# Attention with a top-32 mask, then experts: score tiles as pairs of 64-row products, token rows copied by ScalarE and multiplied by GpSimd

## The chip, the cores and the metric

The kernel runs on one core of a Trainium2 chip. The metric is the time of one execution in device microseconds (us). Five engines work side by side, each through its own instructions in order: PE (TensorE, matrix products), DVE (VectorE), ACT (ScalarE), POOL (GpSimd) and SP (SyncE, which here only issues DMAs). They meet through semaphores. PE reads SBUF and writes PSUM; DVE and ACT read both; POOL works on SBUF alone.

## The reference, cut to what matters

```python
# q, k, v: 8 batches x 8 heads x 576 x 64
scores = scale * np.matmul(q, k.transpose(0, 1, 3, 2))
kth = np.partition(scores, -32, axis=-1)[..., -32:-31]
scores = np.where(scores >= kth, scores, -1e9)
attn = np.exp(scores - scores.max(-1, keepdims=True))
attn = attn / (attn.sum(-1, keepdims=True) + 1e-09)
x = np.matmul(attn, v)            # -> 4608 tokens x 512 (all heads of a token side by side)
logits = x @ w_gate + modality_bias[modality_id]
e_idx = np.argmax(logits, axis=1)                     # one of 8 experts
out = softmax(logits)[e_idx] * (relu(x @ w1[e_idx]) @ w2[e_idx])
```

## The kernel before

Two heads of a batch make a head pair; there are 32 pairs (index p), four to a batch. Rows of scores are worked in tiles of 128 x 576: nine tiles to a pair (index j), 288 in all. Tiles 0 to 7 hold 128 rows of one head, head h = j mod 2, row block c = j div 2. Tile 8 holds the last 64 rows of both heads.

The main loop (L1056) runs over steps i, one new tile in each, and every step issues for many tiles at once: the score products of tile i + 2 (`qk`), the seven sub-maxima of tile i (`subs`, L385), the chain that finds its 24 largest values (`chain`, L396 to L398), the product y = S * sign (`pool_y`, L423, POOL), a last maximum over y (`find`, L427), the exponential (`expo`, L441, ACT), the masked probabilities P (`keep`, L447, DVE), the transposes of P (`trans`, L481) and the products with v (`av`, L509). All of these run in the order in which the step writes them; nothing reorders them.

Scores need more than one pass, since q and k are held as a high part and a low part (`split`, L268: the high part by a copy to fp32r, the low part as what is left). `prep` turns k and q by transposes, and `st` [128, high/low, q/k, 576] then has head 0 on partitions 0 to 63 and head 1 on 64 to 127. Before, ten DMAs per pair (`stack`, L309) build from it `qs` (high above low, 128 partitions, per head) and `ks` (high twice, low twice), so that one product of 128 rows gives (q high + q low) * k high or * k low: four products of 128x288 per tile, two per half of the columns (L371). Tile 8 takes two block-diagonal tiles `qbd`, filled by POOL (`fill`, L322), and eight products of 512 or 64 columns. Pair 0 is worked without stacks (`unstacked`, L341): four terms of 64 rows each, head 0 into PSUM tile S and head 1 into T.

The score tile is copied out of PSUM by ACT (`sevac`, L375), S having one buffer. POOL's `gate` (L468) is a tiny multiplication that reads P, so that y of a step stands behind P of the step before; `below` (L406) is POOL's tiny n.

Experts run beside the attention. Tokens are sorted to experts in slots of 256; 13 slots are worked inside the loop, the others in a tail behind it (L997). How many expert products (L775, L787) a step gets is decided when the program is written, by `spare_pe`: each step adds STEP (3.39) and takes off the entries of COST for what else the step puts on PE, and a refund is added in steps where DVE does `late` work (L1210).

When a batch is done, `xrow` (L538) turns its result back to token rows: for each of five row blocks, four transposes into a PSUM tile X and, in the next step, one DVE multiplication by the factors `RD` (one over the sum of P) into x5. `route` then sends the rows to their experts by indirect DMA on POOL.

## Time and profile before

| | us |
|---|---|
| median of three runs (1263.65 to 1268.3) | 1266.87 |
| the profiled execution | 1262.36 |
| its span, first to last instruction | 1260.6 |
| busy in it: PE / DVE / ACT / POOL | 1181.1 / 1140.2 / 989.0 / 677.8 |
| granted PE clock over the span, as a share of 2.4 GHz | 0.986 |

The profile records start and length of every instruction. PE's ends are modelled, and its products overlap, so the time from the end of one product to the end of the next says what a product costs; its listed length does not. An engine's busy time in a stretch, against the length of the stretch, tells how near to full it is.

### The profile page before, as it was taken

The numbers are of one execution on the slowest core, as the hardware profiler recorded it, in microseconds if no ns is written. First come the engines' busy times: TensorE is split into PE (matmuls) and PEld (weight loads), VectorE is DVE, ScalarE is ACT, GpSimd is POOL, SyncE is SP. The second block draws the span as 40 slices with busy tenths as digits, with TensorE's granted clock in tenths as the row PEclk, the third lists the DMA queues.
The fourth block names the chain that finished last, engine by engine and source line by source line (L and its number), as shares of the span: only waits on it lengthen the run. The fifth ranks groups of instructions, "written<-read, shape, count | busy, mean of one in ns | idle before, by whom it ended". The sixth has DMA issues, their size and how long they took to land. (4 is left out here: it accounts for less than half of the span.)

```text
span 1260.6 us, 28788 instructions
## 1 busy us (share of the span) xinstructions
PE 1181.1 (94%) x8032; PEld 927.0 (74%) x8032; DVE 1140.2 (90%) x5917; ACT 989.0 (78%) x2014; POOL 677.8 (54%) x1253
## 2 busy tenths in 40 slices
PE   7889987899988999989999999999999999999985
PEld 5667766768766868677777778787778775699885
DVE  6999999999999999999999999999999996477751
ACT  4999988889888988888898888888888885256542
POOL 4888865564574557554755466556755573211110
PEclk7999999999999999999999999999999999999998
DMA  4563337754356745655666566656576425478550
GB/s 107 156 186 86 87 86 224 199 150 126 86 136 188 217 117 157 189 156 139 171 184 177 146 182 191 185 154 169 161 207 178 128 71 168 150 251 275 190 174 15
DMA packets 204339, 199.28 MB, mean 158 GB/s; under 512 B 104413, under 2 KB 151533, under 8 KB 204160
## 3 DMA queue, kind: packets, MB, share of 16 engines
q1 hardware_dynamic: 196880, 177.96, 51.2%
q0 software_dynamic: 6080, 19.00, 4.2%
q8 instruction: 69, 1.13, 0.4%
q14 instruction: 110, 0.90, 0.2%
q10 hardware_dynamic: 1200, 0.30, 0.1%
HBM read 118.63 MB, written 24.23 MB: 113 GB/s over the span
## 5 line engine op out<-in xcount | busy, mean ns | idle before, releaser
L385 DVE MAX8 cand<-Ssb 128x8 f32<-128x82 f32 (+1 forms) x2016 | 429.5, 230 | 5.4 <-ACT Ssb L378 5.4
L423 POOL TENSOR_TENSOR y<-Ssb,K 128x576 f32<-128x576 f32 x288 | 370.4, 1286 | 5.7 <-ACT K L417 5.4
L417 ACT ACTIVATE K<-Ssb,n 128x576 bf16<-128x576 f32 x288 | 227.2, 789 | 29.0 <-POOL y L423 28.2
L378 ACT ACTIVATE Ssb<-S 128x576 f32<-128x576 f32 x284 | 185.9, 655 | 80.9 <-PE S L371 45.5
L371 PE MATMUL S<-ks,qs 128*128 128x288 f32 x992 | 220.3, 344 | 29.2 <-ACT Ssb L378 16.8
L427 DVE MAX8 mg<-y 128x8 f32<-128x576 f32 x288 | 214.7, 745 | 10.2 <-POOL y L423 10.2
L371 PEld LDWEIGHTS S<-ks,qs 128*128 128x128 f32 x992 | 151.5, 190 | 73.0 <-ACT Ssb L378 27.3
L775 PE MATMUL E<-xgT,w1b 128*128 128x256 f32 x816 | 196.8, 384 | 8.8 <-ACT hT L779 7.6
L441 ACT ACTIVATE ex<-Ssb,sm 128x576 f32<-128x576 f32 x256 | 199.9, 781 | 0.0
L489 ACT ACTIVATE PT<-T 128x640 f32<-128x640 f32 (+1 forms) x288 | 191.0, 663 | 5.6 <-PE T L481 5.6
L787 PE MATMUL E<-w2b,hT 128*128 128x512 f32 x400 | 188.2, 597 | 1.5 <-ACT hT L779 0.9
L447 DVE SCALAR_TENSOR_TENSOR P<-Ssb,kth,ex 128x576 f32<-128x576 f32 x224 | 188.0, 840 | 0.7 <-DVE cand L385 0.3
L481 PE MATMUL T<-idf,P 128*128 128x128 f32 x1152 | 170.4, 275 | 8.9 <-ACT P L466 8.9
L775 PEld LDWEIGHTS E<-xgT,w1b 128*128 128x128 f32 x816 | 147.5, 190 | 32.8 <-ACT hT L779 11.3
L470 POOL TENSOR_SCALAR spare<-P 1x1 f32<-1x1 f32 x224 | 50.0, 223 | 202.3 <-DVE mg L396 189.2
L481 PEld LDWEIGHTS T<-idf,P 128*128 128x128 f32 x1152 | 135.0, 140 | 17.9 <-ACT P L466 13.5
L509 PE MATMUL X<-PT,vm 128*64 128x256 f32 (+1 forms) x1536 | 145.0, 331 | 1.5 <-ACT xT L512 0.9
L410 POOL TENSOR_SCALAR n<-mg 128x1 f32<-128x1 f32 x288 | 72.8, 253 | 111.5 <-DVE mg L398 103.2
L509 PEld LDWEIGHTS X<-PT,vm 128*64 128x64 f32 x1536 | 88.4, 137 | 47.2 <-issue 10.2
L787 PEld LDWEIGHTS E<-w2b,hT 128*128 128x128 f32 x400 | 69.8, 190 | 59.7 <-issue 53.9
L1027 POOL DMA_INDIRECT out_dram<-ot,tk x12 | 12.0, 1000 | 106.7 <-ACT ot L1026 106.7
L396 DVE MAX8 mg<-cand 128x8 f32<-128x56 f32 x288 | 60.9, 211 | 0.2
(233 smaller groups left out, 2245.1 us busy)
## 6 DMA issues: line engine op xcount, KB each, us to landing
w1b<-in_moe_w_dram SPq DMA_DIRECT2D x76, 512.0 KB, 5.4
w2b<-in_moe_w_dram SPq DMA_DIRECT2D x76, 512.0 KB, 5.3
ks<-st SPq DMA_DIRECT2D x62, 288.0 KB, 3.4
qs<-st SPq DMA_DIRECT2D x124, 144.0 KB, 2.7
ks<-st SPq DMA_DIRECT2D x62, 256.0 KB, 4.8
xg<-xs SPq DMA_DIRECT2D x19, 516.0 KB, 5.1
km<-in_k_dram SPq DMA_DIRECT2D x64, 128.0 KB, 3.4
vm<-in_v_dram SPq DMA_DIRECT2D x32, 256.0 KB, 3.4
```

What stands on the lines that cost most here:

```text
L371: PE.matmul(ps[:, hf, u - a:v - a], l, d["ks"][:, x, h, u + o:v + o], start=(n == 0), stop=(n == len(terms) - 1), skip_group_check=(j == 8))
L385: return [lambda s=s: V.max(c[:, s * 8:s * 8 + 8], T[i]["S"][:, bnd[s]:bnd[s + 1]]) for s in range(NSUB)]
L417: A.activation(t["K"], t["S"], AF.Sign, scale=2.0 ** -24 - 1.0, bias=t["n"][:, 1, i % 3:i % 3 + 1], accum_out=t["n"][:, 0, i % 3:i % 3 + 1])
L423: G.tensor_tensor(t["y"], t["S"], t["K"], op=OP.mult)
L427: V.max(t["mg"][:, i % 3, 24:32], t["y"])
L441: A.activation(t["ex"], t["S"], AF.Exp, bias=t["s"][:, i % 3:i % 3 + 1])
L447: V.scalar_tensor_tensor(t["P"], t["S"], kth[:, i:i + 1], t["ex"], op0=OP.is_ge, op1=OP.mult, accum_out=dn)
L481: PE.transpose(T[i]["pt"][:, x, :], (Pm if c == 4 else Pb[c % 2])[:, h * 512 + x * 128:h * 512 + x * 128 + 128], idf)
L489: A.activation(o, T[i]["pt"][:, :n], AF.Copy)
L509: PE.matmul(o.rearrange("p (a b) -> p a b", a=2) if j < 8 else o, l, r, start=(c == 0), stop=(c == 4))
L775: PE.matmul(ps[:, f % 2], w1b[:, c, f * 128:(f + 1) * 128], xgT[:, c, :], start=(c == 0), stop=(c == KC - 1))
L787: PE.matmul(o["py"], hT[:, f, t * 128:(t + 1) * 128], w2b[:, f, :], start=(f == 0), stop=(f == FC - 1))
```

## The change

Three things change. First, `stack` goes. `qk` reads `st` itself, 64 rows at a time, and adds three terms (high*high, high*low, low*high) in place of four. The two halves of the columns (index g) go to the two halves of the rows: the half with g = h from `st`, where the head lies, the other from `sw`, a copy of that head's q and half of its k on the other partitions, made by five DMAs per pair (`cross`). Each tile then has six products of 64x288, alternating between the row halves. Tile 8 takes one `qbd` with high and low and six products of 128x288. `st` gets two buffers; pair 0 uses the same code, with three terms in `unstacked` and tile 8 through `qk`.

Second, for batches 1 to 6 `xrow` has ACT copy the turned rows out of PSUM to x5 and puts two multiplications of 128x256 in place on a list, `halves`, from which POOL takes one per step. The other two batches keep DVE's multiplication.

Third, COST of `qk` goes from 0.5 to 0.4 and of `mix` (tile 8) from 1.02 to 0.8.

```diff
--- before.py
+++ after.py
@@ -51,7 +51,7 @@
 PB = (2, 4, 6)
 AV3 = (0, 5)
 AV7 = (0, 5)
-COST = {"trans": 0.5, "qk": 0.5, "mix": 1.02, "rest": 0.22, "t": 0.11, "prep": 0.43, "logits": 1.2, "xrow": 0.54, "av": 0.49, "av8": 0.17}
+COST = {"trans": 0.5, "qk": 0.4, "mix": 0.8, "rest": 0.22, "t": 0.11, "prep": 0.43, "logits": 1.2, "xrow": 0.54, "av": 0.49, "av8": 0.17}
 RN = 6
 QO = 0
 PJ0 = (1, 2, 3)
@@ -112,6 +112,7 @@
     xs = dr.tile([ZROW + SLOT, XW], FT, name="xs")
 
 
+    TERMS = ((0, 0), (0, 1), (1, 0))
     LD, PR, T = {}, {}, {}
     PAUSE = lambda: None
 
@@ -170,10 +171,9 @@
     G.iota(tokc[:, 0:4], pattern=[[1, 4]], base=0, channel_multiplier=4, allow_small_or_imprecise_dtypes=True)
     G.iota(tokc[:, 4:5], pattern=[[1, 1]], base=512, channel_multiplier=1, allow_small_or_imprecise_dtypes=True)
 
-    qbd = [[o.tile([128, 128], FR, name=f"qbd{i}{j}", bufs=1) for j in range(2)] for i, o in enumerate((const, wk))]
-    for a in qbd:
-        for t in a:
-            V.memset(t.bitcast(FT), 0.0)
+    qbd = [o.tile([128, 2, 128], FR, name=f"qbd{i}", bufs=1) for i, o in enumerate((const, wk))]
+    for t in qbd:
+        V.memset(t.bitcast(FT), 0.0)
     Pb = [wk.tile([128, 2 * S], FT, name=f"P{i}", bufs=1) for i in range(2)]
     Pm = const.tile([128, 640], FT, name="Pm")
     G.memset(Pm[:, S:], 0.0)
@@ -263,6 +263,7 @@
 
 
     late, late_pe = [], []
+    halves = deque()
     nxt = deque()
 
     def split(hi, lo, ps, first=False):
@@ -281,10 +282,8 @@
 
 
         d = PR.setdefault(p, {})
-        if first:
-            d.setdefault("st", st0)
-        elif "st" not in d:
-            d["st"] = wk.tile([128, 2, 2, S], FR, name="st", bufs=1)
+        if "st" not in d:
+            d["st"] = wk.tile([128, 2, 2, S], FR, name="st", bufs=2)
         if part == "t":
             ps = psX.tile([128, 2, 64], FT, name="X")
             PE.matmul(ps.rearrange("p x s -> p (x s)"), LD[p]["kq"].rearrange("p h d -> p (h d)"), idf, start=True,
@@ -302,27 +301,26 @@
 
         half = lambda x: slice(x * 64, x * 64 + 64)
         if part == "k":
-            d["ks"] = wk.tile([128, 2, 2, S], FR, name="ks", bufs=2)
-        else:
-            d["qs"] = wk.tile([128, 2, S], FR, name="qs", bufs=2)
-
-        def stack(h, queues=(SP, SP)):
-            for v in range(2):
-                if part == "k":
-                    for a, b, o in ((0, S, 0),) if h == 0 else ((0, 512, 64), (512, S, -512)):
-                        queues[v].dma_start(d["ks"][half(v), :, h, a + o:b + o].bitcast(FT), st[half(h), :, a:b].bitcast(FT))
-                else:
-                    queues[v].dma_start(d["qs"][half(v), h, :].bitcast(FT), st[half(h), v, :].bitcast(FT))
+            d["sw"] = wk.tile([128, 2, 512 + 288], FR, name="sw", bufs=2)
+
+        def cross(h):
+
+            if part == "q":
+                cols = ((0, 512, 0),)
+            else:
+                cols = ((288, S, 512),) if h == 0 else ((512, S, 512), (0, 224, 576))
+            for a, b, o in cols:
+                SP.dma_start(d["sw"][half(1 - h), :, o:o + b - a].bitcast(FT), st[half(h), :, a:b].bitcast(FT))
 
         for h in range(2):
-            f = lambda h=h, **o: stack(h, **o)
+            f = lambda h=h: cross(h)
             f.move = True
             late_pe.append(f)
 
     def fill(p, bd):
         for h in range(2):
-            G.tensor_scalar(bd[h][:, h * 64:h * 64 + 64], PR[p]["qs"][:, h, 512:].bitcast(FT), 1.0, 1.0,
-                            op0=OP.mult, op1=OP.mult)
+            r = slice(h * 64, h * 64 + 64)
+            G.tensor_scalar(bd[r, :, r], PR[p]["st"][r, :, 1, 512:].bitcast(FT), 1.0, 1.0, op0=OP.mult, op1=OP.mult)
 
     def flush():
         for x in (late, late_pe, nxt):
@@ -330,52 +328,42 @@
                 f()
             x.clear()
 
-    st0 = wk.tile([128, 2, 2, S], FR, name="ks", bufs=2)
-    bd0 = wk.tile([128, 2, S], FR, name="qs", bufs=2)[:, 0, :256].rearrange("p (x s) -> p x s", x=2)
-
-    def fill_first():
-        for h in range(2):
-            r = slice(h * 64, h * 64 + 64)
-            G.tensor_scalar(bd0[r, :, r], PR[0]["st"][r, :, 1, 512:].bitcast(FT), 1.0, 1.0, op0=OP.mult, op1=OP.mult)
-
     def unstacked(j):
 
         if j % 2:
             return
-        ps = [psS.tile([128, 2, 512], FT, name="S"), psT.tile([128, 2, 512], FT, name="T")][:1 + (j < 8)]
+        ps = [psS.tile([128, 2, 512], FT, name="S"), psT.tile([128, 2, 512], FT, name="T")]
+        st = PR[0]["st"]
         for h, t in enumerate(ps):
             T[j + h] = {"ps": t[:, :, :288]}
-        st = PR[0]["st"]
-        r = [slice(h * 64, h * 64 + 64) if j < 8 else slice(0, 128) for h in range(2)]
-        for x in range(2):
-            for y in range(2):
-                for h, a, b, o in ((0, 0, 288, 0), (1, 0, 64, 512), (1, 64, 288, -64), (0, 288, S, 0), (1, 288, S, -64)):
-                    if h < len(ps):
-                        l = bd0[:, x, :] if j == 8 else st[r[h], x, 1, j * 64:j * 64 + 128]
-                        PE.matmul(ps[h][:, a // 288, a % 288:a % 288 + b - a], l, st[r[h], y, 0, a + o:b + o],
-                                  start=(x + y == 0 and a % 288 == 0), stop=(x + y == 2), skip_group_check=True)
+        for x, y in TERMS:
+            for h, a, b, o in ((0, 0, 288, 0), (1, 0, 64, 512), (1, 64, 288, -64), (0, 288, S, 0), (1, 288, S, -64)):
+                r = slice(h * 64, h * 64 + 64)
+                PE.matmul(ps[h][:, a // 288, a % 288:a % 288 + b - a], st[r, x, 1, j * 64:j * 64 + 128],
+                          st[r, y, 0, a + o:b + o], start=(x + y == 0 and a % 288 == 0), stop=(x == 1),
+                          skip_group_check=True)
 
     def qk(i, p, j, bd):
+
         d = PR[p]
+        st = d["st"]
         ps = psS.tile([128, 2, 512], FT, name="S")
-        for hf in range(2):
-            a, b = (hf * 288, hf * 288 + 288) if j < 8 else ((0, 512), (512, S))[hf]
-            if j < 8:
-                c, h = divmod(j, 2)
-                terms = [(d["qs"][:, h, c * 128:(c + 1) * 128], x, h, a, b, 0) for x in range(2)]
-            else:
-                terms = [(bd[0], x, 0, a, b, 0) for x in range(2)]
-                for u, v, o in ((a, min(b, 512), 64), (512, b, -512)):
-                    terms += [(bd[1], x, 1, u, v, o) for x in range(2)] if u < v else []
-            for n, (l, x, h, u, v, o) in enumerate(terms):
-                PE.matmul(ps[:, hf, u - a:v - a], l, d["ks"][:, x, h, u + o:v + o], start=(n == 0),
-                          stop=(n == len(terms) - 1), skip_group_check=(j == 8))
-        T[i] = {"ps": ps[:, :, :288] if j < 8 else ps.rearrange("p a b -> p (a b)")[:, :S]}
+        c, h = divmod(j, 2)
+        for x, y in TERMS:
+            for g in range(2):
+                r = slice(g * 64, g * 64 + 64)
+                if j == 8:
+                    l, m = bd[:, x, :], st[:, y, 0, g * 288:g * 288 + 288]
+                elif g == h:
+                    l, m = st[r, x, 1, c * 128:c * 128 + 128], st[r, y, 0, h * 224:h * 224 + 288]
+                else:
+                    l, m = d["sw"][r, x, c * 128:c * 128 + 128], d["sw"][r, y, 512:]
+                PE.matmul(ps[:, g, :288], l, m, start=(x + y == 0), stop=(x == 1), skip_group_check=True)
+        T[i] = {"ps": ps[:, :, :288]}
 
     def sevac(i):
         T[i]["S"] = sb = wk.tile([128, S], FT, name="Ssb", bufs=LR + 1 + QL - QO)
-        ps = T[i]["ps"]
-        A.activation(sb.rearrange("p (a b) -> p a b", a=2) if len(ps.shape) == 3 else sb, ps, AF.Copy, scale=0.125)
+        A.activation(sb.rearrange("p (a b) -> p a b", a=2), T[i]["ps"], AF.Copy, scale=0.125)
 
     bnd = [(x * S) // NSUB for x in range(NSUB + 1)]
 
@@ -540,6 +528,20 @@
         ps = psX.tile([128, HP, 128], FT, name="X")
         for hp in range(HP):
             PE.transpose(ps[:n_, hp, :], xTb[hp][:, c * 128:c * 128 + n_], idf)
+        if FAST <= u < B - 1:
+            o = x5b[:n_, c, :Dm]
+            def weigh(a):
+                y = o.rearrange("p (a d) -> p a d", d=D)[:, a:a + HP, :]
+                w = RD[u][:n_, :, 2 * c:2 * c + 2]
+                w = w[:, a // 2:a // 2 + HP // 2, :]
+                y = y.rearrange("p (a h) d -> p a h d", h=2)
+                G.tensor_tensor(y, y, w[:, :, :, None].to_broadcast([n_, HP // 2, 2, D]), op=OP.mult)
+
+            def out_of():
+                A.activation(o, ps[:n_].rearrange("p a d -> p (a d)"), AF.Copy)
+                halves.extend(lambda a=a: weigh(a) for a in (0, HP))
+            xev.append(out_of)
+            return
         late.append(lambda: V.tensor_tensor(
             x5b[:n_, c, :Dm].rearrange("p (a h d) -> p a h d", a=HP, h=2),
             ps[:n_].rearrange("p a (h d) -> p a h d", h=2),
@@ -912,7 +914,6 @@
         for _ in range(2 * n):
             PE.matmul(ps[:, :256].rearrange("p (a b) -> p a b", a=2), onesb, onesb[:, None, :].to_broadcast([128, 2, 128]), start=True, stop=True)
 
-    V.memset(bd0.bitcast(FT), 0.0)
     keep_warm(KW)
     bd_ = const.tile([128, 4], FT, name="bad")
     badi = const.tile([1, 1], I32, name="badi")
@@ -934,7 +935,7 @@
 
     for part in "kqt":
         prep(0, part, True)
-    fill_first()
+    fill(0, qbd[0])
     modality = bias_loads()
     for nm in "kq":
         if NPAIR > 1:
@@ -948,7 +949,6 @@
     dn_of = lambda u: den[(u // 36) % 2][:, (u // 9) % HP, u % 9:u % 9 + 1]
     PREP, PREP0 = dict(zip(PJ, "tkq")), dict(zip(PJ0, "tkq"))
     two = lambda nm, shape: [wk.tile(shape, FR, name=nm + x) for x in "hl"]
-    TERMS = ((0, 0), (0, 1), (1, 0))
     turn = [0]
 
     def acc(shape):
@@ -1067,7 +1067,7 @@
         def scores():
             if ok(i + QL):
                 pp, jj = divmod(i + QL, 9)
-                if pp == 0:
+                if pp == 0 and jj < 8:
                     unstacked(jj)
                 else:
                     qk(i + QL, pp, jj, qbd[pp % 2])
@@ -1232,6 +1232,8 @@
             pool_y(i - LY)
         if ok(i - 1):
             below(i - 1)
+        if halves:
+            halves.popleft()()
         if ok(i - 2) and (i - 2) % 3 == 2:
             small(i - 4)
         if j == 3 and 0 < p < NPAIR:
```

On PE, at tile 8 of a pair and the tile after it, among the row blocks of batch 2 (E are expert products, T the transposes of P), before:

```order
L775 MATMUL E<-xgT,w1b 128x256 x6
L371 MATMUL S<-ks,qbd_117 128x512 x2
L371 MATMUL S<-ks,qbd_118 128x512 x2
L371 MATMUL S<-ks,qbd_117 128x64 x2
L371 MATMUL S<-ks,qbd_118 128x64 x2
L481 MATMUL T<-idf,P_124 128x128 x4
L787 MATMUL E<-w2b,hT 128x512 x2
L371 MATMUL S<-ks,qs 128x288 x4
L481 MATMUL T<-idf,P_124 128x128 x5
```

The same place now:

```order
L777 MATMUL E<-xgT,w1b 128x256 x6
L361 MATMUL S<-st,qbd_116 128x288 x6
L469 MATMUL T<-idf,P_120 128x128 x4
L789 MATMUL E<-w2b,hT 128x512 x2
L361 MATMUL S<-st 128x288
L361 MATMUL S<-sw 128x288
L361 MATMUL S<-st 128x288
L361 MATMUL S<-sw 128x288
L361 MATMUL S<-st 128x288
L361 MATMUL S<-sw 128x288
L469 MATMUL T<-idf,P_120 128x128 x5
```

The expert products and transposes stand where they stood; the tile's four products have become six that alternate between `st` and `sw`, with products of all 128 rows on both sides.

On POOL, in the steps of the first row blocks of batch 1 (spare<-P is `gate`, sm a small copy for the exponential), before:

```order
L470 TENSOR_SCALAR spare<-P_123 1x1
L423 TENSOR_TENSOR y<-Ssb,K 128x576
L410 TENSOR_SCALAR n<-mg 128x1
L404 TENSOR_SCALAR sm<-mg 128x3
L802 DMA out_dram<-ot,stok_134 4608x512
L526 MEMSET spare 1x1
L470 TENSOR_SCALAR spare<-P_124 1x1
L423 TENSOR_TENSOR y<-Ssb,K 128x576
L410 TENSOR_SCALAR n<-mg 128x1
```

And now, in steps of that batch:

```order
L458 TENSOR_SCALAR spare<-P_119 1x1
L411 TENSOR_TENSOR y<-Ssb,K 128x576
L398 TENSOR_SCALAR n<-mg 128x1
L538 TENSOR_TENSOR x_152<-x_152,rd 128x256
L392 TENSOR_SCALAR sm<-mg 128x3
L458 TENSOR_SCALAR spare<-P_120 1x1
L411 TENSOR_TENSOR y<-Ssb,K 128x576
L398 TENSOR_SCALAR n<-mg 128x1
L538 TENSOR_TENSOR x_152<-x_152,rd 128x256
```

Each half stands between n of its step and the `gate` of the next.

## Rows read from the trace of the kernel before

**Rows 1.** Windows: us, busy by engine (instructions), clock share, DMA share, GB/s.

```profile
50.00:293.00 243.00, 215.54 (x1681) 169.27 (x1678) 240.43 (x1339) 215.48 (x469) 170.44 (x269) 1.00 0.56 149
293.00:428.00 135.00, 124.05 (x888) 97.74 (x889) 130.95 (x723) 116.48 (x240) 76.69 (x147) 1.00 0.55 146
428.00:562.00 134.00, 129.89 (x861) 99.68 (x859) 132.91 (x726) 115.01 (x236) 76.62 (x149) 0.99 0.58 160
562.00:695.00 133.00, 131.51 (x875) 101.57 (x870) 130.14 (x708) 114.50 (x236) 79.06 (x151) 1.00 0.63 173
695.00:826.00 131.00, 129.82 (x867) 100.03 (x865) 128.36 (x701) 113.93 (x235) 78.76 (x151) 1.00 0.62 170
826.00:959.00 133.00, 131.49 (x879) 101.64 (x878) 130.05 (x708) 115.58 (x239) 80.37 (x155) 1.00 0.63 172
959.00:1045.00 86.00, 83.26 (x553) 62.83 (x553) 83.63 (x453) 70.37 (x143) 51.96 (x100) 1.00 0.46 130
```

**Rows 2.** Timeline of PE, full clock: start, length, operation, count.

```profile
639.67 1.89 PE L775 MATMUL E<-xgT,w1b 128*128 128x256 f32 x8
641.21 0.88 PE L371 MATMUL S<-ks,qs 128*128 128x288 f32 x4
641.92 0.71 PE L481 MATMUL T<-idf,P 128*128 128x128 f32 x5
...
651.20 0.29 PE L509 MATMUL X<-PT,vt 128*64 128x64 f32 x4
651.42 0.80 PE L371 MATMUL S<-ks,qs 128*128 128x288 f32 x4
...
1045.83 0.29 PE L509 MATMUL X<-PT,vt 128*64 128x64 f32 x4
1046.05 0.76 PE L481 MATMUL T<-idf,P 128*128 128x128 f32 x5
```

**Rows 3.** Timeline of PE, pair 0's 64-row products.

```profile
21.73 0.85 PE L297 MATMUL X<-idf,qm 128*128 128x128 f32 x3
22.51 0.61 PE L355 MATMUL S<-ks 64*128 64x288 f32 x1
...
23.16 0.44 PE L355 MATMUL S<-ks 64*128 64x288 f32 x1
...
23.34 0.25 PE L355 MATMUL T<-ks 64*128 64x64 f32 x1
23.40 0.44 PE L355 MATMUL S<-ks 64*128 64x288 f32 x1
...
24.41 0.97 PE L355 MATMUL T<-ks 64*128 64x288 f32 x4
25.31 0.50 PE L276 MATMUL X<-st,nid 128*128 128x512 f32 x1
```

**Rows 4.** Windows, the stretch of most of rows 3.

```profile
17.00:25.00 8.00, 7.31 (x43) 6.15 (x41) 6.63 (x45) 4.61 (x10) 3.01 (x6) 0.50 0.13 27
```

**Rows 5.** Timeline of PE, tile 8 of a pair.

```profile
767.17 1.89 PE L775 MATMUL E<-xgT,w1b 128*128 128x256 f32 x8
768.71 1.64 PE L371 MATMUL S<-ks,qbd 128*128 128x512 f32 x8
```

**Rows 6.** Groups by line from 293 to 1007 us, and of the span (POOL).

```profile
L543 DVE TENSOR_TENSOR x<-X,rd 128x512 f32<-128x512 f32 (+1 forms) x30 | 20.1, 671 | 1.6 <-PE X L542 1.6
...
L779 ACT ACTIVATE hT<-E 128x512 f32<-128x512 f32 x40 | 24.1, 602 | 8.0 <-PE E L775 7.4
...
L423 POOL TENSOR_TENSOR y<-Ssb,K 128x576 f32<-128x576 f32 x288 | 370.4, 1286 | 5.7 <-ACT K L417 5.4
```

**Rows 7.** Lines L447 and L410: duration ns min/median/max, first and last start.

```profile
L447 DVE SCALAR_TENSOR_TENSOR P<-Ssb,kth,ex x224: 787/802/1932, 36.9 to 1056.4; 128x576 f32<-128x576 f32 x112
...
L410 POOL TENSOR_SCALAR n<-mg x288: 192/193/978, 16.8 to 1045.9; 128x1 f32<-128x1 f32 x144
```

**Rows 8.** Waits from 300 to 600 us: total, times, longest.

```profile
PE S L371 <- DMA qs<-st: 3.7, 2, 2.9
```

## The prediction

> **What bounds the kernel now.** I read the busy times by stretch first [rows 1], cut where the batch cycles fall: 36 score tiles (four head pairs of nine) take 131 to 135 us. Two engines are close to full, and they change places. From 50 to 293 us DVE is busy 240.4 of 243 us and PE only 215.5. From 293 to 562 DVE still leads (131.0 of 135, then 132.9 of 134). From 562 to 959, three cycles, PE leads: 131.5 of 133, 129.8 of 131, 131.5 of 133, with DVE idle 2.6 to 3.0 us in each. So in these 397 us whatever is added to PE is added to the span, and what DVE sheds is not gained. After 1045 us comes the expert tail, which the change leaves alone. The chain of waits that ended last reaches back into that tail alone, so it says nothing on the edit. The profiled execution took 1262.4 us (span 1260.6), 4.5 us under the median of 1266.9; I add the sum to both.
>
> **Score products, tiles 0 to 7 of a pair.** Before: four products of 128 rows and 288 columns. The end of a block of four lies 0.53 us behind the end of the product ahead of it (639.67 + 1.89 = 641.56, then 641.21 + 0.88 = 642.09), so 0.13 us each [rows 2]. After: six products of 64 rows, in three pairs. Do the two halves of a pair run at once? Tiles of pair 0 show it, at half clock [rows 3, 4]: two products of S start at 23.16 and 23.40, 0.24 us apart, which is 288 columns at 1.2 GHz, and one of T starts at 23.34 on the other rows, while the first of them still runs. They overlap, so three pairs cost 0.40 us at full clock if the pitch of 0.13 holds: 0.13 saved per tile.
>
> But the array must change its shape, and that has a price wherever the trace shows it. Behind the products with P (shape 128*64) the same block of four ends 0.73 us after them, not 0.53 (651.20 + 0.29 = 651.49, 651.42 + 0.80 = 652.22): 0.20 for going in [rows 2]. Five transposes end 0.54 us behind a block of their own shape (642.09 to 642.63), and 0.69 behind shape 128*64 (1046.12 to 1046.81): 0.15 for going out [rows 2]. That 64*128 pays as well is seen at both ends of pair 0's blocks: the first product starts at 22.51, only 0.07 before the transposes ahead of it end (22.58), and L276 at 25.31, 0.07 before the last one ends (25.38), at full clock and 0.43 us end to end, while blocks of one shape start 0.35 or 0.17 ahead of that end [rows 2 to 4]. I take 0.20 and 0.15, the rows at full clock; bounds are 0 (a change of row groups alone is free) and 0.20 each. In the new order every such block is followed by transposes of full shape, so it pays both. Per tile: 0.20 + 0.15 - 0.13 = +0.22 us of PE. The 33 blocks that stand right behind products with P in the whole program (some 3 in 32) paid for the way in before: +0.02.
>
> By the Trainium skill, "TensorE: Matmul & The Clock Gate", section "Measured speedup vs the span model", concurrent tiles take one product's time plus some 4 ns for each further tile, and it names no charge for coming and going. By that alone a tile would be 0.13 us cheaper; the rows at 651 and 1046 speak against it, and it is weighed as the first rival.
>
> **Tile 8 of a pair.** Before, eight products, four of 512 and four of 64 columns, end 1.29 us behind the product ahead (767.17 + 1.89 = 769.06 to 770.35) [rows 5]. After, six full-shape products of 288, 6 x 0.13 = 0.80. That saves 0.49 us. Per cycle PE gains or loses 29 x 0.22 + 3 x 0.02 - 4 x 0.49 = **+4.5 us** (bounds -6.1 without a price for shapes, +6 with 0.20 both ways).
>
> **The lower planner costs** move hardly any work: the refund for rows done late by DVE goes too. In the built order the expert products reach the same count at the same tile (576 when the last score tile's transposes are through, within 2 all the way), 13 slots before the tail in both. I cost this at nothing.
>
> **Rows to tokens.** For six of eight batches DVE loses 30 multiplications, 20.1 us at 671 ns, all between 293 and 1007 [rows 6]: 3.4 us per cycle. ScalarE gets 30 copies of 128x512 at about 0.60 us [rows 6], 3.0 us per cycle, with 17 to 19 us idle there; they free the PSUM tile a little earlier than DVE did. GpSimd gets 60 multiplications of 128x256; its 128x576 takes 1.29 us, so 0.57 by columns to 1.29 at most, I take 0.65: 6.5 us per cycle, with over 50 us idle. Queued behind a half on GpSimd are the next step's gate and y; GpSimd mostly waits there for DVE, so I count nothing.
>
> Yet these halves may meet DVE's P instruction. It takes 787 ns at best, 802 in the median and up to 1932, and GpSimd's tiny n takes 193 in the median and up to 978 [rows 7]: something holds both up now and then, and they read the same memory at the same time. Each half stands right behind n, so a third of the 60 may catch a P, half of 0.65 each: 6.5 us back, 1.1 per cycle. Net DVE: -2.3 per cycle (bounds -3.4 and +3.1, when each of ten halves holds P for 0.65).
>
> The Trainium skill, "SBUF — State Buffer", section "Who interferes with whom", says that a DVE instruction with two SBUF inputs and a GpSimd one that reads SBUF block each other for the whole instruction; the spread of n and P is what that would look like. It is the ground of the second rival.
>
> **Transfers.** Ten copies per pair (four of 144 KB among them) become five, 800 KB instead of 1728. PE waited for qs 3.7 us between 300 and 600 [rows 8]; I count 3 gained on PE, where DVE leads. st has two buffers now, and a pair's last reader is through before its buffer is written again.
>
> **The sum**, by stretch, from PE's and DVE's busy times [rows 1]. 0 to 50: three terms for four in pair 0's products (0.24 us each at half clock): -1 (0 to -3). 50 to 293: DVE leads and keeps its work, PE's +8 fit into 27 idle: 0 (0 to +3). 293 to 428: DVE leads: -2 (-3.4 to 0). 428 to 562: PE comes to 129.9 + 4.5 - 3 = 131.4, DVE to 130.6; from 134 to 132.5: -1.5 (-3 to 0). The three cycles from 562: PE +4.5, less 1 of the 1.2 to 1.5 us that it idles now: +3.5 each (5 to 13 together). 959 to 1045: 2.7 us of PE against 2.7 idle, of which I let it use a quarter: +2 (0 to 3). Sum **+8 us** (-4 to +19): 1270.5 in a run like the profiled one, 1275 against the median.
>
> **Rivals.** First, row groups change without a price. For it: only rows are grouped, columns stay whole. Against it: the starts 0.07 us before an end at 22.51 and 25.31. Then PE sheds 6.1 per cycle, DVE leads everywhere and gives 2.3 to 3.4 in each of 5 cycles, 2 in the rest, 1 at the start: about -18, **1249**. Second, on the slow side: GpSimd's halves hold P. Its place is DVE's P instruction at the end of a step; its price is up to 60 x 0.65 = 39 us on DVE, against 20 saved; it decides as soon as over half the halves start within 0.65 us ahead of a P. DVE then leads again in the early cycles: +18 there in place of -3.5, less what PE hides later, about +19, **1286**. Third, at full clock the two halves take turns: 0.40 us more per tile, 11.6 per cycle of 29 such tiles, on PE everywhere from 293 on: about +60, **1327**. Fourth, PE's lead after 562 is softer than its busy time says (its ends are modelled), and DVE's relief shows: **1262**.
>
> **Chances.** Forecast 0.66; first rival 0.12, second 0.10, third 0.05, fourth 0.07. This kernel's measurement tells 0.5% (6.3 us) from no change. The forecast's own spread puts 0.36 of its 0.66 over that, 0.28 within and 0.02 below; second and third are slower, the first faster, the fourth half same and half faster. Slower 0.51, same 0.31, faster 0.18. The range leaves out the first and the third rival: 1260 to 1290.
>
> **What would show it.** Transposes after a score block ending 0.69 us behind it and the block's first pair 0.33 behind what is ahead; pairs starting together, 0.13 us apart; PE busy over 98% from 562 to 959 in cycles of 135 to 137 us, with DVE idle 5 to 7 us in each; cycles from 293 to 562 shorter by 1 to 3. P's median near 0.80 clears the second rival. Transposes 0.54 behind a block would prove me wrong on the main term.

## The result, and the profile after

The changed kernel takes 1275.45 us (median of five runs, 1274.02 to 1279.62) against 1265.97 us for the kernel before (five runs, 1263.1 to 1268.3): a ratio of 1.0081, with a 95% interval of 1.0059 to 1.0103. It is slower by 9.5 us; forecast were 8. The profiled execution took 1274.02 us, its span is 1272.3 us (before: 1262.36 and 1260.6).

First the busy times by stretch, the view of [rows 1], now cut where ScalarE's first row copy of each batch starts (before it was about where DVE's first row multiplication starts; columns as there):

```profile
50.00:291.60 241.60, 218.28 (x1764) 157.34 (x1765) 240.28 (x1331) 215.27 (x467) 168.04 (x267) 0.99 0.43 118
291.60:423.60 132.00, 124.45 (x915) 88.31 (x913) 126.53 (x700) 114.94 (x238) 82.78 (x152) 0.97 0.42 114
423.60:558.40 134.80, 131.75 (x915) 89.93 (x914) 131.31 (x729) 116.81 (x242) 85.47 (x162) 1.00 0.46 131
558.40:694.40 136.00, 135.61 (x934) 94.16 (x933) 131.49 (x720) 117.86 (x243) 88.34 (x162) 1.00 0.49 141
694.40:830.90 136.50, 134.99 (x929) 93.12 (x928) 131.59 (x700) 117.55 (x244) 86.23 (x162) 1.00 0.49 138
830.90:967.30 136.40, 134.89 (x929) 93.08 (x928) 131.42 (x700) 117.47 (x244) 86.18 (x162) 1.00 0.49 138
967.30:1055.00 87.70, 85.50 (x585) 58.95 (x585) 83.02 (x431) 73.32 (x150) 58.55 (x108) 1.00 0.37 108
```

From 558 on PE is busy 98.9 to 99.7% of the time in cycles of 136.0 to 136.5 us. DVE should have had 129 - 2.3 us of work per cycle; it shows 131.5, so what the rows saved was spent again. Who waits for whom has changed too. These are DVE's waits over one late cycle (tiles 227 to 263; us in total, times, longest), before and then after:

```profile
DVE mg L427 <- POOL y L423: 1.9, 4, 0.6
DVE P L447 <- DVE cand L385: 0.3, 1, 0.3
```

```profile
DVE lt L573 <- PE X L565: 2.1, 1, 2.1
DVE mg L415 <- POOL y L411: 2.0, 4, 0.6
```

Before, no wait for PE is named. After, DVE waits once in the cycle for PE's transposes of a finished batch's logits.

Next the timeline of PE around a score block behind an expert product, to be laid beside the first three lines of [rows 2] (start, length, operation, count):

```profile
640.82 1.03 PE L777 MATMUL E<-xgT,w1b 128*128 128x256 f32 x4
641.78 0.40 PE L361 MATMUL S<-sw 64*128 64x288 f32 x1
641.78 0.40 PE L361 MATMUL S<-st 64*128 64x288 f32 x1
642.01 0.29 PE L361 MATMUL S<-sw 64*128 64x288 f32 x1
642.02 0.29 PE L361 MATMUL S<-st 64*128 64x288 f32 x1
642.15 0.29 PE L361 MATMUL S<-sw 64*128 64x288 f32 x1
642.16 0.29 PE L361 MATMUL S<-st 64*128 64x288 f32 x1
642.38 0.76 PE L469 MATMUL T<-idf,Pm 128*128 128x128 f32 x5
...
770.40 1.89 PE L777 MATMUL E<-xgT,w1b 128*128 128x256 f32 x8
771.94 1.15 PE L361 MATMUL S<-st,qbd 128*128 128x288 f32 x6
```

The expert products end at 641.85, the first pair at 642.18 (0.33 later), the third at 642.45 (0.60); the five transposes end at 643.14, 0.69 behind the block. The two products of a pair start within 0.01 us of each other, and the pairs end some 0.13 us apart. Tile 8 ends at 773.09, 0.80 us behind the product ahead of it (772.29).

Then single lines of the program (duration in ns: least, median, most; first and last start), to be laid beside [rows 7], and the idle time of GpSimd ahead of its halves:

```profile
L435 DVE SCALAR_TENSOR_TENSOR P<-Ssb,kth,ex x224: 786/806/1955, 33.2 to 1066.3; 128x576 f32<-128x576 f32 x112
...
L398 POOL TENSOR_SCALAR n<-mg x288: 190/191/740, 16.7 to 1055.8; 128x1 f32<-128x1 f32 x144
...
L538 POOL TENSOR_TENSOR x<-x,rd x60: 609/616/1284, 293.0 to 1023.3; 128x256 f32<-128x256 f32 x48, 64x256 f32<-64x256 f32 x12
...
its engine sat idle before it (us, times) until:
  ACT x L541: 28.7, 16
```

P's median has hardly moved (802 to 806 ns), and a half takes 0.62 us. What was not expected is the last line: 16 of the 60 halves kept GpSimd waiting for ScalarE's copy, 28.7 us in all.

### The profile page after: what moved, and what is told of

Its sections match the earlier page's. It is cut to its first block, busy times and chain, and to the rows that moved or that the text cites. A ratio compares the mean times of both kernels' runs of the same rounds, so it can differ in the third digit from the quotient of the medians.

```text
span 1272.3 us, 29402 instructions
## 1 busy us (share of the span) xinstructions
PE 1204.8 (95%) x8438; PEld 869.9 (68%) x8438; DVE 1142.7 (90%) x5884; ACT 1005.5 (79%) x2044; POOL 722.3 (57%) x1313
## 5 line engine op out<-in xcount | busy, mean ns | idle before, releaser
L373 DVE MAX8 cand<-Ssb 128x8 f32<-128x82 f32 (+1 forms) x2016 | 430.7, 230 | 2.0 <-ACT Ssb L366 1.9
L777 PE MATMUL E<-xgT,w1b 128*128 128x256 f32 x816 | 198.7, 387 | 7.2 <-ACT hT L781 5.4
L435 DVE SCALAR_TENSOR_TENSOR P<-Ssb,kth,ex 128x576 f32<-128x576 f32 x224 | 197.5, 882 | 0.5 <-ACT PT L477 0.2
L469 PE MATMUL T<-idf,P 128*128 128x128 f32 x1152 | 181.0, 284 | 11.8 <-ACT P L454 11.3
L361 PE MATMUL S<-st 64*128 64x288 f32 x744 | 166.0, 329 | 11.6 <-ACT Ssb L366 11.2
L777 PEld LDWEIGHTS E<-xgT,w1b 128*128 128x128 f32 x816 | 148.3, 191 | 32.0 <-ACT hT L781 9.6
L361 PE MATMUL S<-sw 64*128 64x288 f32 x744 | 165.0, 329 | 5.4 <-ACT Ssb L366 2.8
L469 PEld LDWEIGHTS T<-idf,P 128*128 128x128 f32 x1152 | 124.2, 141 | 53.7 <-issue 26.1
L361 PEld LDWEIGHTS S<-st 64*128 64x128 f32 x744 | 107.2, 186 | 64.5 <-ACT Ssb L366 21.0
L361 PEld LDWEIGHTS S<-sw 64*128 64x128 f32 x744 | 107.1, 187 | 43.3 <-issue 17.0
```

What stands on the lines that cost most here:

```text
L361: PE.matmul(ps[:, g, :288], l, m, start=(x + y == 0), stop=(x == 1), skip_group_check=True)
L373: return [lambda s=s: V.max(c[:, s * 8:s * 8 + 8], T[i]["S"][:, bnd[s]:bnd[s + 1]]) for s in range(NSUB)]
L435: V.scalar_tensor_tensor(t["P"], t["S"], kth[:, i:i + 1], t["ex"], op0=OP.is_ge, op1=OP.mult, accum_out=dn)
L469: PE.transpose(T[i]["pt"][:, x, :], (Pm if c == 4 else Pb[c % 2])[:, h * 512 + x * 128:h * 512 + x * 128 + 128], idf)
L777: PE.matmul(ps[:, f % 2], w1b[:, c, f * 128:(f + 1) * 128], xgT[:, c, :], start=(c == 0), stop=(c == KC - 1))
```

## One table of all kernels

The experiments are read by the same marks in every trace: the start of the first sub-maximum on DVE (seven per tile, L373 after, L385 before) of tiles 155, 191, 227, 263 and 287, counted from 0. Tiles 155 to 263 are the three cycles in which the prediction let PE lead. "Rest" runs from tile 287 to the end of the span. "Ahead" is how long a tile's scores had lain ready in SBUF when DVE began on them, at tiles 155, 191 and 227. Two places where it is read, tile 227 before and after (timelines of ACT and DVE):

```profile
812.05 0.65 ACT L378 ACTIVATE Ssb<-S 128x576 f32<-128x576 f32 x1
...
819.18 0.23 DVE L385 MAX8 cand<-Ssb 128x8 f32<-128x82 f32 x1
```

```profile
816.31 0.67 ACT L366 ACTIVATE Ssb<-S 128x576 f32<-128x576 f32 x1
...
819.78 0.23 DVE L373 MAX8 cand<-Ssb 128x8 f32<-128x82 f32 x1
```

Before, 819.18 - 812.70 = 6.5 us ahead; after, 819.78 - 816.98 = 2.8. No tile from 155 to 286 finds its scores missing in either kernel (the least time ahead is 3.7 us before and 0.7 after), so where PE holds DVE up is at the logits.

| kernel | median us | ratio to before, 95% interval | 155-191 | 191-227 | 227-263 | 263-287 | rest | ahead |
|---|---|---|---|---|---|---|---|---|
| before | 1265.97 | | 132.5 | 131.9 | 132.2 | 89.5 | 219.6 | 6.1, 6.5, 6.5 |
| after | 1275.45 | 1.0081 (1.0059 to 1.0103) | 132.3 | 136.5 | 136.4 | 94.6 | 221.5 | 6.7, 2.8, 2.8 |
| qk_only | 1270.30 | 1.0038 (1.0024 to 1.0051) | 132.2 | 135.0 | 134.9 | 92.6 | 222.6 | 6.1, 4.2, 4.3 |
| x_only | 1265.61 | 1.0001 (0.9988 to 1.0015) | 132.0 | 133.9 | 132.3 | 90.0 | 221.9 | 6.1, 3.5, 5.0 |
| tiny128 | 1276.55 | 1.0080 (1.0049 to 1.0111) | 133.2 | 134.9 | 134.7 | 92.4 | 221.7 | 5.4, 4.1, 4.3 |
| tiny64 | 1303.43 | 1.0299 (1.0270 to 1.0327) | 141.6 | 139.8 | 139.7 | 96.7 | 222.3 | 0.1, 2.5, 2.5 |
| eight | 1268.31 | 1.0028 (1.0014 to 1.0042) | 134.1 | 131.9 | 131.9 | 89.5 | 221.6 | 4.2, 6.5, 6.5 |
| eight_x | 1266.96 | 1.0017 (0.9999 to 1.0034) | 133.8 | 132.3 | 131.3 | 88.6 | 222.6 | 5.7, 4.5, 6.1 |
| no_halves | 1270.67 | 1.0052 (1.0034 to 1.0070) | 132.8 | 135.3 | 135.3 | 92.3 | 222.7 | 6.5, 2.8, 2.8 |
| halves_late | 1274.93 | 1.0100 (1.0073 to 1.0127) | 132.5 | 135.6 | 135.6 | 93.8 | 221.5 | 6.7, 2.8, 2.9 |
| old_cost | 1271.14 | 1.0050 (1.0033 to 1.0066) | 129.8 | 135.1 | 132.4 | 89.4 | 232.5 | 7.3, 2.8, 1.9 |
| x_fewer | 1266.53 | 1.0018 (1.0000 to 1.0037) | 129.7 | 130.6 | 129.7 | 89.1 | 229.2 | 7.6, 4.5, 2.8 |

The rest is 2 us shorter in the profile of before than in every other with the same expert slots, though no edit touches that part, so some 2 us of a comparison of these spans is put down to scatter.

## Experiment: the two halves of the change, each alone

x_only is the kernel before with the new rows: ScalarE copies, GpSimd multiplies. The experts stand where they stood.

```diff
+        if FAST <= u < B - 1:
+            ...
+            xev.append(out_of)
+            late.append(lambda: None)
+            return
```

> The kernel before with the new way of the token rows alone (ScalarE copies, GpSimd halves); the scores and every expert product stay where they were. If PE leads from 562 us on and DVE before that: DVE's relief shows only in the two cycles from 293 to 562, 2 to 3 us each, and hardly behind: 1260 to 1264 against 1266 before. If GpSimd's halves hold DVE's P instruction for long (second rival): slower, up to 1285. If PE's lead is soft (fourth rival): the relief of 20 us shows for the most part, 1248 to 1254.

qk_only is the changed kernel with DVE's row multiplication and the old planner costs; the experts stand as in the kernel before.

```diff
-COST = {"trans": 0.5, "qk": 0.4, "mix": 0.8, ...
+COST = {"trans": 0.5, "qk": 0.5, "mix": 1.02, ...
...
-        if FAST <= u < B - 1:
-            ...
-            return
```

> The change without the new token rows and with the old planner costs, so that every expert product stands in the step where it stood before: 64-row score products alone. If the array's change of shape costs 0.20 in and 0.15 out: +3.5 to 4.5 us in each of the three cycles from 562, +1 to 3 from 428 to 562 and behind 959, 0 earlier: 1276 to 1281 against 1266. If coming and going were free, PE would shed 6 us per cycle, and with DVE as it was the time would stay or fall: 1258 to 1266.

x_only: 1265.61 us, no change (0.9988 to 1.0015), and not the few us gained that I wrote down. qk_only: 1270.30 us, slower by 0.24 to 0.51%, less than expected. So the scores cost about 5 us, the rows alone nothing, and both together 9.5: beside the new scores the rows, with the planner's numbers, cost some 5 us more. One full late cycle (windows, tiles 227 to 263, within 1 us; columns as in [rows 1]) of before, then of qk_only, then of x_only:

```profile
819.20:951.40 132.20, 130.69 (x872) 100.86 (x872) 129.25 (x704) 114.78 (x237) 79.61 (x152) 1.00 0.62 171
```

```profile
817.70:952.60 134.90, 134.17 (x929) 92.93 (x928) 129.67 (x704) 115.67 (x236) 79.54 (x152) 1.00 0.49 139
```

```profile
820.50:952.80 132.30, 130.77 (x873) 100.92 (x872) 128.53 (x700) 116.17 (x242) 87.22 (x162) 1.00 0.62 171
```

qk_only adds 3.5 us to PE's busy time (130.69 to 134.17) and 2.7 to the cycle. In x_only PE has the work of before, DVE 0.7 us less, and the cycle is the same.

## Experiment: the price of the shape by itself

tiny64 is the kernel before with one product of 64 rows and 16 columns ahead of every score block of tiles 0 to 7, pairs 1 to 31. tiny128 has the same product with 128 rows.

```diff
     def qk(i, p, j, bd):
...
+        if j < 8:
+            PE.matmul(ps[:, 0, :16], onesb[:64, :], onesb[:64, :16], start=True, stop=True, skip_group_check=True)
```

> The kernel before, with one more product in front of each block of four score products of tiles 0 to 7 of pairs 1 to 31: 64 rows, 16 columns, into columns that the next product overwrites. It adds no work to speak of, but the array must go to shape 64*128 and back. If a change of shape costs about 0.2 us each way: 0.4 us per tile, 13 us per cycle of PE, +2 from 293, +9 from 428, +13 in each of three cycles, +6 behind and some 3 ahead: about 1325. If the price belongs to columns groups or to the 288-column products and not to the shape: like the next kernel, 1267 to 1275.

> The same with 128 rows in the small product: no change of shape. One more weight load and product of some 0.06 us per tile, 2 us per cycle where PE leads: 1269 to 1275 against 1266, whichever theory holds; the difference to the kernel with 64 rows is the price of the shape alone.

1303.43 and 1276.55 us: 27 us lie between two kernels whose only difference is the number of rows of a product that does next to nothing. The timelines of PE, tiny64 and then tiny128:

```profile
822.74 0.60 PE L767 MATMUL X<-idf,xg 128*128 128x128 f32 x4
823.27 0.18 PE L362 MATMUL S<-onesb 64*128 64x16 bf16 x1
823.38 0.81 PE L373 MATMUL S<-ks,qs 128*128 128x288 f32 x4
```

```profile
821.69 0.38 PE L777 MATMUL E<-xgT,w1b 128*128 128x256 f32 x1
821.91 0.17 PE L362 MATMUL S<-onesb 128*128 128x16 bf16 x1
821.94 0.79 PE L373 MATMUL S<-ks,qs 128*128 128x288 f32 x4
```

With 64 rows the block ends 0.85 us behind what is ahead of it (823.34 to 824.19), with 128 rows 0.66 (822.07 to 822.73). Over the blocks behind a product of full shape that ran without a gap from 293 us on (some 146 in each trace) the medians from there to the end of the first transpose are 0.949 and 0.752 us: 0.20 us for going into the 64-row shape and out again. It is less than the 0.35 that the kernel after pays, and why is not shown; but that rows alone have a price is shown, and the first rival is out. The control cost more than I wrote down, 0.11 us for each small product in place of 0.06. And 29 x 0.11 = 3.2 us more on PE per cycle made the late cycles longer by 2.5 to 3.0: what is added to PE there shows almost in full, as in qk_only.

## Experiment: take work off PE

eight is the kernel before, with tile 8 at 1728 columns in seven full-shape products in place of 2304 in eight. The 64 lower rows of the second operand for the low part of K now hold the other head, so that one product serves both heads.

```diff
-                terms = [(bd[0], x, 0, a, b, 0) for x in range(2)]
-                for u, v, o in ((a, min(b, 512), 64), (512, b, -512)):
-                    terms += [(bd[1], x, 1, u, v, o) for x in range(2)] if u < v else []
+                terms = [(bd[:, 0:128], 0, 0, a, b, 0)]
+                for u, v, o in ((a, min(b, 512), 64), (512, b, -512)):
+                    terms += [(bd[:, 64:192], 0, 1, u, v, o)] if u < v else []
+                terms.append((bd[:, 192:320], 1, 0, a, b, 0))
```

> The kernel before, all products at 128 rows and every tile j < 8 as it is; only tile 8 of pairs 1 to 31 is scored by 1728 columns in 7 products in place of 2304: the two products with the low part of K become one, since the second row half of that operand now holds the other head's rows. One more small transfer and one more piece per pair on SyncE's queue. If the shapes alone are the price of the change and tile 8's columns its gain, tile 8's block falls by 0.4-0.5 us, four times a cycle: 1.8 us in each of three TensorE-led cycles, some in the others: 1256-1262. If VectorE (busy 129 to 130 of 131 to 133 us there) or the transfers take over at once: 1263-1267.

eight_x adds the rows of x_only to it.

> The same with ScalarE's copies and GpSimd's multiplications of the middle batches' rows. If the relief of VectorE (2.3 us per cycle at best) was worth nothing alone only because TensorE led, it shows now that TensorE is shorter too: 1253-1259, 2 to 5 us below the one without. If P takes it back as in the changed kernel (4 us per cycle of excess), no gain over the one without, or a loss of 1-3 us.

Neither gains: 1268.31 us (1.0014 to 1.0042, a shade slower than expected by either theory) and 1266.96 (0.9999 to 1.0034). Tile 8 did become shorter, by 0.4 us (timeline of PE in eight; the block ends at 776.26, 0.89 us behind 775.37, against 1.29 in [rows 5]):

```profile
773.48 1.89 PE L785 MATMUL E<-xgT,w1b 128*128 128x256 f32 x8
775.02 1.24 PE L381 MATMUL S<-ks,qbd 128*128 128x288 f32 x7
```

And the late cycle of eight in the windows:

```profile
824.60:956.40 131.80, 129.31 (x868) 99.69 (x868) 129.19 (x704) 114.41 (x237) 80.16 (x156) 1.00 0.62 172
```

PE is busy 129.31 us, 1.4 less than before, and the cycle is as long as before. PE is idle 2.5 us in it, for 1.5 before. Nor has the time that the scores lie ready changed (6.5 us, table): DVE sets this pace. In x_only, where DVE has less to do, the cycle is the same 132.3, now with PE ahead by only 5.0. So in the kernel before PE and DVE are in step to within half a microsecond in 132; taking from one of them gives nothing. With both relieved (eight_x) the two late cycles are 132.3 and 131.3. What eight loses lies mostly earlier: tiles 11 to 83 take 248.1 us against 244.4, tiles 155 to 191 134.1 against 132.5. Why is not shown.

## Experiment: what the rows cost beside the new scores

no_halves is the kernel after without GpSimd's multiplications. Its rows lack the factors.

```diff
-                halves.extend(lambda a=a: weigh(a) for a in (0, HP))
```

> The changed kernel without GpSimd's in-place multiplications by the factors (60 of 0.61 us); the output leaves the factors out. Theory A, they are what the row part costs (a half waits for ScalarE's copy, pushes GpSimd's y back, and y meets the next P): the last full cycles fall from 136.4 to 134.5-135, P's excess over 0.80 us falls from about 4 to about 1 us per cycle, and the time from 1275.4 to 1268-1271, at or below the score part alone (1270.3). Theory B, ScalarE's copies are what costs (they stand ahead of the evictions that TensorE waits for): the time stays at 1274-1276 and the cycles at 136.

halves_late takes each half one step later.

```diff
+        ready_halves = len(halves)
...
-        if halves:
+        if ready_halves:
             halves.popleft()()
```

> The changed kernel with each multiplication on GpSimd taken one step later, so that ScalarE's copy is long done when GpSimd reaches it; nothing is left out. Theory A1, the price is the wait of the first half of each pair for the copy (up to 2.4 us) that pushes the gate and y behind it: GpSimd's idle time before the halves falls from 28.7 us to under 5, P's excess in the late cycles from 4 to about 1.5 us per cycle, the time to 1270-1273. Theory A2, any half beside P on the vector engines costs the same wherever it stands: excess and time stay (1274-1276).

no_halves: 1270.67 us, as the first theory had it, and as qk_only: the halves are what the rows cost, not ScalarE's copies. How they cost by the first theory is seen once in the kernel after, in the timelines of GpSimd and DVE at the start of a late cycle:

```profile
831.57 0.61 POOL L538 TENSOR_TENSOR x<-x,rd 128x256 f32<-128x256 f32 x1 [2.45 <-ACT x L541]
...
832.41 0.18 POOL L458 TENSOR_SCALAR spare<-P 1x1 f32<-1x1 f32 x1
832.56 1.27 POOL L411 TENSOR_TENSOR y<-Ssb,K 128x576 f32<-128x576 f32 x1
...
832.69 1.75 DVE L435 SCALAR_TENSOR_TENSOR P<-Ssb,kth,ex 128x576 f32<-128x576 f32 x1
```

The half waits 2.45 us for the copy; gate and y queue behind it; y then starts 0.13 us ahead of the next P, and P takes 1.75 us in place of 0.80. The Trainium skill, "SBUF — State Buffer", section "Who interferes with whom", has such a pair block each other; here P ends 0.61 us behind the end of y, 0.19 short of a full block. Summed over a late cycle, P stands 3.9 us over 0.80 per instruction in the kernel after, 0.7 in qk_only: this is where DVE's saved 3.4 us went.

But that sum does not need the halves. Without them, in no_halves, it is 3.6 us, where the first theory had about 1. Over the whole span it is 22.1 us there, 18.9 in the kernel after and 9.6 before. In no_halves most of it stands at tiles 244 to 247; at the first of these y comes late behind a DMA that GpSimd issues (GpSimd, then DVE):

```profile
884.57 0.97 POOL L601 DMA_INDIRECT xs<-x,dest  x1 [0.20 <-issue]
...
885.86 1.28 POOL L411 TENSOR_TENSOR y<-Ssb,K 128x576 f32<-128x576 f32 x1
...
885.74 2.02 DVE L435 SCALAR_TENSOR_TENSOR P<-Ssb,kth,ex 128x576 f32<-128x576 f32 x1
```

So the time came out as the first theory had it, and its path did not: P is long where y runs beside it, with or without the halves.

halves_late takes the wait away (no idle time of GpSimd ahead of any half, 28.7 us before), P's excess falls to 1.8 us per cycle, as that theory said, and the late cycles from 136.45 to 135.6. But the time is 1274.93 us, not 1270 to 1273. Its late cycle and that of no_halves (windows):

```profile
821.60:957.20 135.60, 134.56 (x928) 93.04 (x927) 129.12 (x699) 117.44 (x242) 85.92 (x162) 1.00 0.49 139
```

```profile
818.40:953.70 135.30, 134.54 (x928) 93.09 (x928) 130.54 (x700) 117.48 (x242) 79.88 (x152) 1.00 0.49 139
```

DVE is busy 129.1 us in the one and 130.5 in the other, and the one with the busier DVE is the shorter: P's excess is not what sets these cycles. PE is busy 134.5 us in both, and the length goes by the rest of its time: idle 1.5 us in the kernel after (busy 134.9), 1.0 in halves_late, 0.8 in no_halves. Of it the profile names the wait of an expert product for ScalarE's hT: 0.9, 0.5 and 0.2 us in this cycle. So from tile 191 on, in one trace of each kernel, the halves cost 2.5 us by being early (halves_late's three stretches, 2 x 0.85, and 94.6 to 93.8), and about 2 more by being there at all (to no_halves, 2 x 0.3 and 93.8 to 92.3). The medians bear out the sum (1275.45 to 1270.67) and not its parts, since halves_late is only 0.5 us below the kernel after: the profiled halves_late starts 1.4 us later (tile 0 at 11.4 us for 10.0, where both programs are alike) and takes 0.8 more over tiles 83 to 119. How the halves delay hT by way of ScalarE is left open.

## Experiment: the planner's two numbers

old_cost is the kernel after with the two numbers of before. The planner then places one expert slot fewer in the loop (its trace has 768 products with w1 on L777, that of the kernel after 816) and one more behind it.

```diff
-COST = {"trans": 0.5, "qk": 0.4, "mix": 0.8, ...
+COST = {"trans": 0.5, "qk": 0.5, "mix": 1.02, ...
```

> The changed kernel with the table's two old numbers (0.5 and 1.02): the planner then places one expert slot fewer in the loop (576 instead of 624 products by step 300) and one more behind it. Theory: the two numbers only keep the experts where the kernel before has them, so undoing them lengthens the part behind the loop by 25-28 us and takes about as much work off TensorE in the loop, where only the stretches that TensorE leads (the last three) give it back, 10-20 us: 1283-1292. Rival: TensorE's work in the loop was worth its full time, and the tail takes the slot at the same price: 1272-1279.

x_fewer is x_only without `late.append(lambda: None)`, and so without the refund that the planner got for a late row; its expert products stand as in old_cost.

```diff
             xev.append(out_of)
-            late.append(lambda: None)
             return
```

> The kernel before with ScalarE's copies and GpSimd's multiplications, and with the refund that DVE's late rows gave the planner left away too, so that one expert slot fewer stands in the loop (576 products by step 300, exactly as in old_cost). From old_cost the slot is worth 11 us behind the loop, and TensorE loses 3 to 4 us of work per cycle. Theory, VectorE leads as soon as TensorE is a little shorter (as in eight): the cycles fall only by the 1-2 us that VectorE is relieved by, 4-8 us in all, and the tail's 11 stay: 1268-1272. Rival, TensorE led in the last three cycles of the kernel before: 12-16 us back for 11: 1259-1264.

old_cost: 1271.14 us, below both expectations and 4.3 us below the kernel after. Its runs (1267.8 to 1272.2) and those of the kernel after (1274.0 to 1279.6) don't meet, though the intervals of the two ratios do by a little. The rest is 11 us longer (table: 232.5 for 221.5), not 25 to 28, and the stretches from tile 83 to 287 shorter by 17. The late cycle (tiles 227 to 263) and the part behind the loop:

```profile
811.90:944.20 132.30, 131.48 (x940) 92.08 (x937) 130.92 (x699) 117.80 (x244) 84.12 (x160) 1.00 0.49 142
1033.60:1266.10 232.50, 214.08 (x1367) 183.56 (x1365) 144.53 (x401) 111.49 (x179) 37.67 (x81) 0.97 0.52 175
```

PE is 3.4 us less busy than in the kernel after and the cycle 4.1 shorter; the cycle ahead of it (tiles 191 to 227) is 1.4 shorter. So beside the new scores PE does set the pace. x_fewer makes the same move in a kernel with the old scores: 1266.53 us, no change by our bound (1.0000 to 1.0037). The time lies between the two expectations. From tile 119 on its cycles fall by 1.3 to 2.8 us (the theory had 1 to 2), and the rest takes it back (229.2 for 219.6). So moving a slot behind the loop paid in the kernel where PE leads alone, and not in the one where DVE and PE are level. No version here beats the kernel before.

## Why the prediction was right, and where its steps were not

**The time.** 1275 forecast, 1275.45 measured; the sign and the main mechanism, the price of the shape, hold. That the figure is met to half a microsecond is luck: 9.5 us were measured for 8, on a base that five runs put 0.9 below that of the three. By stretch (tile marks, after less before) the parts are less even than the sum:

| stretch | forecast | measured |
|---|---|---|
| to tile 11 (0 to 41 us) | -1 | -3.6 |
| tiles 11 to 83 | 0 | +0.8 |
| 83 to 119, 119 to 155 | -2, -1.5 | -0.6, -0.3 |
| 155 to 191 | +3.5 | -0.2 |
| 191 to 227, 227 to 263 | +3.5 each | +4.6, +4.2 |
| 263 to 287 | +2 | +5.1 |
| rest | 0 | +1.9, scatter |

Of the 3.6 us at the start, 1.4 lie ahead of tile 0, whose mark stands at 9.3 to 11.4 us in the five kernels that begin as the changed one does; they are put down to scatter too.

**Score products: right.** 0.33, 0.13 apart, and 0.69 out, as foretold. Over the same kind of blocks the median from the product ahead to the end of the first transpose goes from 0.640 to 0.853 us, +0.21 for +0.22, and from 0.839 to 0.852 behind products with P (+0.02 foretold; these are 25 of 248 blocks in the trace, not 33, which is the 3 in 32 that the sum took). Tile 8: 0.80 as worked out; with its way out it is 0.55 shorter, for 0.49. On PE's busy time a late cycle of qk_only is 3.5 us longer, for 4.5. That the two halves of a pair run at once is shown too, at full clock; the third rival is out.

**"PE leads from 562": wrong as stated.** I read it from busy shares (98.9% against 98%). The 6.5 us for which scores lie ready in every late cycle of the kernel before, and eight, show DVE setting the pace with PE level, and the profile names no wait of DVE for PE in these three cycles; in the kernel after it names 1.6 to 2.1 us in each. For work that is added the two readings give nearly the same, which is why the sum came out; the difference is the stretch 155 to 191. There the program first used up what PE was ahead: 6.7 us fall to 2.8, so 3.9 us of PE's extra work don't show. From tile 191 on they show, as tiny128 confirms with other work (ahead 5.4 to 4.1; +0.7, then +3.0 and +2.5).

**Rows: the relief was worth nothing, as written; its price was missed.** A half takes 0.62 us (0.65 taken), P's median stayed, and over the span P stands 9.3 us more over 0.80 than before (6.5 foretold, 39 by the second rival), so that rival in its strong form is out. The wrong step was to let a half cost nothing but DVE's time: against no_halves the halves cost 1.1 us in each late cycle and 2.3 in 263 to 287, while P's excess is as large without them. They wait for the copy, which I did not reckon with ("I count nothing" for what is queued behind a half), but taking that wait away left the time where it was; by which path they cost stays open. That term, and DVE's missing gain from 285 to 555, were balanced by the cycle that showed nothing.

**Planner costs: right against the kernel before, blind beside it.** The placement is the same for most of the loop (at tiles 128 to 144 the trace after stands up to 16 expert products behind that of before, elsewhere within 4, and not within 2 as I had it), and no_halves, with the same numbers, is as fast as qk_only, so nothing was to be added; but the old numbers would have moved a slot out of the loop, at a gain of some 4 us.

**Transfers.** 199.3 MB fell to 169.9, and PE's wait for operands between 300 and 600 us [rows 8] is gone; the 3 us counted show on no stretch, since DVE sets the pace there.

## What to carry to other kernels

Before halving the rows of a product to run two at once, count how often the array goes into that shape and out: here 0.35 us for every block against 0.13 won inside it, so the shape pays only where many such products stand in a row. Busy shares don't tell which of two nearly full engines sets the pace; who waits for whom does, and how long one's results lie ready for the other. Here, where the two were level, work added to PE showed almost in full, while work taken off either showed not at all. And a long wait on an engine off the path need not be the price: without the 28.7 us for which GpSimd waited, the time stayed, and without the halves it fell by 4.8 us while P's excess stayed. Before a path is called the cause, check it in the kernel that leaves the suspected work out.

## What was not expected of the hardware

A bf16 product of 128 rows and 16 columns costs 0.11 us of PE in this order (0.752 against 0.640 us), nearly as much as one of 288 columns (0.13), and the same with 64 rows costs 0.31. GpSimd's multiplication of 128x256 takes 0.616 us where its 128x576 takes 1.27, so nearly by columns. An instruction of 0.80 us on DVE took 1.75 beside a GpSimd instruction of 1.27 that had started 0.13 us ahead of it.
